# Issuing the first wave of loads without the three holds on SyncE's queue

## The chip, the core and the metric

The kernel runs on one core of one Trainium2 chip. Such a core has TensorE (PE, the matmul engine), VectorE (DVE), ScalarE (ACT), GpSimd (POOL) and SyncE (SP), which run side by side and wait for one another through semaphores, and 16 DMA engines that move the data. SP and ACT each issue loads on a queue of their own: q1 in the profile is SP's, q10 is ACT's. The metric is the time of one execution on the device in microseconds, as the median of several runs.

## The reference

One transformer layer on a sequence of 2048 rows of width 512, all in bf16:

```python
h = x + A(layernorm(x))          # A: attention over 8 earlier positions, 2 apart; 32 heads of 16
out = h + B(layernorm(h))        # B: (relu(h @ W_gate) * (h @ W_up)) @ W_down, F = 1376
```

In A, `x @ wqkv` gives queries, keys and values. Row s looks at the keys of the rows s, s-2, ..., s-14, takes a softmax over these eight, sums the values with it, and the result is multiplied with `wo`. The layernorms have no weights.

## The kernel before

The 2048 rows are cut into four chunks of 512 (`tk` 0 to 3), and a chunk into four blocks of 128 rows, so that x consists of 16 blocks, x_0 to x_15; chunk 1 is x_4 to x_7. Each chunk goes through the same stages:

- Layernorm. DVE takes the statistics of each of the four blocks (`bn_stats`, L468, and `bn_aggr`, L471). ACT makes the reciprocal deviation from them (L481, L485). For chunks 1 to 3 DVE makes a bias (L489) and ACT scales the four blocks (L500); for chunk 0 DVE scales (L503). TensorE transposes the blocks (L532) and ACT copies the transposed ones out of the accumulator banks (L548). In chunk 3 four DMA transposes on SP's queue do this instead (L521).
- Queries, keys and values. L573 multiplies the transposed chunk with the weights: 12 steps of four matmuls, for q, k and v and four tiles each. ACT casts the results from the banks to SBUF (L581). In chunk 0 the first six steps are cut into smaller parts, so that they can begin as soon as single blocks of x are there.
- Logits. DVE multiplies queries with shifted keys (L639 in chunk 0, in eight pieces; L624 in the others), TensorE sums over the width of a head (L630), ACT takes the exponential (L688), DVE masks the beginning of the sequence in chunk 0 (L691). SP broadcasts the weights over the partitions with eight DMAs per chunk (L748).
- Values. DVE multiplies them with the weights (L795 in chunk 0, L780 in the others) and adds up (L783 and the lines after it, with POOL's adding DMAs, L823). Then follow the output projection (L861, with `wo`), the second layernorm, the gated network (L934 with the gate and up weights, L984 with the down weights) and the store.

The chunks are interleaved: TensorE works on one chunk's matmuls while DVE works on the attention of another. The order is written out by hand. Each step is an `Op` with an engine, and `Plan.add` gives it the next entry of the list `RANK`; `Plan.order` sorts each engine's steps by rank, so the list fixes the order of the 758 steps on each engine. Every engine then goes through its own list in that order, and a step that waits holds up all the steps behind it. `XT` and `WT` are the times at which the planner believes the loads to land; with a written-out rank they do not change an engine's order, only the choice among the buffers of a kind.

What matters here is `setup` (L312). It first issues chunk 0's loads in turn on SP's and ACT's queue: x_0 and x_2 and the first and third quarter of the q and k weights on SP, x_1 and x_3 and the other two quarters on ACT (L318, L319). Then GpSimd builds small constants (L321 to L330). Then come three holds, and behind each of them loads on SP's queue:

```python
nc.gpsimd.tensor_copy(out=x_sm[0:1, BPC:2 * BPC, 0:1], in_=x_sm[0:1, 3, 0:BPC])
for j in range(BPC, 2 * BPC):
    nc.sync.dma_start(x_sm[:, j:j + 1, :], x_rows[:, j:j + 1, :])
```

The copy reads four elements of x_3 and writes one into each of x_4 to x_7. So it waits until x_3 has landed, and the loads of x_4 to x_7 (L335) wait for the copy, as they write the same places. The second hold (L336) reads the last quarter of the q and k weights and writes an element of the v weights, which holds the v weights' load (L337). The third (L338) reads x_7 and writes an element of x_8, which holds x_8 to x_11 and, behind them on the queue, x_12 to x_15 (L340), the output weights (L342) and the gate weights (L310, two halves). The up and down weights are issued much later, behind a hold of their own (L841).

One more rule of the program counts: its loads from SP and ACT take eight completion semaphores in turn. A load therefore is not issued before the load eight places ahead of it has landed.

Of the kernel before, what the change touches and what calls it, by code (L numbers as in the profile page):

```python
# [17 lines left out]
RANK = [  # L18
# [38 lines left out]
]  # L57


# [143 lines left out]
def kernel(  # L203
# [11 lines left out]
    nc = tc.nc  # L215
# [23 lines left out]
    BPC = CS // P  # L239
# [25 lines left out]
    x_sm = sb.tile([P, NTB, D], BF16, name="x_sm")  # L265
    wqk_sb = sb.tile([P, NT, 2 * D], BF16, name="wqk_sb")
    wv_sb = sb.tile([P, NT, D], BF16, name="wv_sb")
# [44 lines left out]
    def setup():  # L312

        w3_r = A_wqkv.rearrange("(dt p) f -> p dt f", p=P)
        for i in range(2):
            for n, q in enumerate((nc.sync, nc.scalar)):
                j = 2 * i + n
                q.dma_start(x_sm[:, j:j + 1, :], x_rows[:, j:j + 1, :])  # L318
                q.dma_start(wqk_sb[:, j:j + 1, :], w3_r[:, j:j + 1, 0:2 * D])  # L319
        nc.scalar.preload_act_table_set("natural_log_exp_and_others")  # L320
        V.memset(warm[:], 0.0)  # L321
        make_identity(nc, identity[:])
        nc.gpsimd.memset(eps_t[:], EPS)
        nc.gpsimd.iota(ci[:], pattern=[[0, 1]], base=0, channel_multiplier=1)
        nc.gpsimd.iota(sel_i[:], pattern=[[1, H]], base=0, channel_multiplier=0)
        nc.gpsimd.iota(sp_i[:], pattern=[[1, H], [0, DQ]], base=0, channel_multiplier=0)
        nc.gpsimd.iota(sm_i, pattern=[[0, 4], [1, H]], base=0, channel_multiplier=0)
        nc.gpsimd.iota(mk_i[:], pattern=[[1, PADL]], base=0, channel_multiplier=0)
        nc.gpsimd.memset(kT[:, :, 0:PADL], 0.0)
        nc.gpsimd.memset(vT[:, :, 0:PADL], 0.0)  # L330


        nc.gpsimd.tensor_copy(out=x_sm[0:1, BPC:2 * BPC, 0:1], in_=x_sm[0:1, 3, 0:BPC])
        for j in range(BPC, 2 * BPC):
            nc.sync.dma_start(x_sm[:, j:j + 1, :], x_rows[:, j:j + 1, :])  # L335
        nc.gpsimd.tensor_copy(out=wv_sb[0:1, 0, 0:1], in_=wqk_sb[0:1, 3, 0:1])  # L336
        nc.sync.dma_start(wv_sb[:], w3_r[:, :, 2 * D:3 * D])  # L337
        nc.gpsimd.tensor_copy(out=x_sm[0:1, 2 * BPC, 0:1], in_=x_sm[0:1, 2 * BPC - 1, 0:1])  # L338
        for tk in range(2, NCK):
            nc.sync.dma_start(x_sm[:, tk * BPC:(tk + 1) * BPC, :], x_rows[:, tk * BPC:(tk + 1) * BPC, :])  # L340

        nc.sync.dma_start(wo_sb[:], A_wo.rearrange("(p t) f -> p t f", t=NT))  # L342
        for n in "gud":
            for i in range(2):
                if n not in LATE:
                    f_load(n, i)


        for n, (op, by) in enumerate(((ALU.arith_shift_right, 2), (ALU.bitwise_and, H - 1),
                                      (ALU.arith_shift_right, 5))):  # L350
            V.tensor_scalar(out=tmp[:, n:n + 1], in0=ci[:], scalar1=by, scalar2=None, op0=op)
        V.tensor_copy(out=cf[:, 0:3], in_=tmp[:])
        V.tensor_scalar(out=cf[:, 2:3], in0=cf[:, 2:3], scalar1=1.0 * DIL, scalar2=None, op0=ALU.mult)
        V.tensor_scalar(out=cf[:, 3:4], in0=cf[:, 2:3], scalar1=4.0 * DIL, scalar2=None, op0=ALU.add)
        V.tensor_scalar(out=sel[:], in0=sel_i[:], scalar1=cf[:, 0:1], scalar2=None, op0=ALU.is_equal)
        V.tensor_scalar(out=spread[:], in0=sp_i[:], scalar1=cf[:, 1:2], scalar2=None, op0=ALU.is_equal)
        V.tensor_scalar(out=same[:], in0=sm_i, scalar1=cf[:, 1:2], scalar2=None, op0=ALU.is_equal)
        for hf in range(2):
            V.tensor_scalar(out=mask[:, hf, :], in0=mk_i[:], scalar1=cf[:, 2 + hf:3 + hf],
                            scalar2=None, op0=ALU.is_ge)  # L360
# [13 lines left out]
    NWARM, NFILL = 46, (8, 0, 0)  # L374
    NHALF = 6
    QA, QC = 6, 3
    XT = (3.5, 3.65, 5.6, 6.1, 8.5, 8.9, 9.4, 9.9, 15.9, 17.4)
    WT = (7.55, 7.55, 5.0, 14.2, 18.7, 25.5, 22.0, 29.0)
    DMAT = (('h',2,0),('h',2,2),('h',3,0),('h',3,2),('h',1,0),('x',3,0),('x',3,2))

    EARLY = (1, 2, 3)
# [689 lines left out]
```

## Time and profile before

| what | value |
|---|---|
| median of three runs (lowest to highest) | 196.97 us (196.93 to 197.28) |
| the profiled execution's own time | 197.36 us |
| its span, first to last instruction | 195.5 us |
| mean granted TensorE clock | 1.00 of full speed |
| busy: PE, DVE, ACT, POOL | 189.1, 147.2, 118.9, 18.6 us |
| read from and written to HBM | 8.42 MB, 2.10 MB |

All moments below are microseconds from the start of the span. What ends a matmul is modelled, so that "busy" on PE includes filling and draining; the pitch from one matmul to the next says how fast it works: 0.216 us for 512 columns, 0.056 us for 128. The profile gives for each load when it was issued and how long it took until it had landed:

| load | issued | landed | | load | issued | landed |
|---|---|---|---|---|---|---|
| x_1 (ACT) | 0.74 | 3.79 | | x_5 | 7.02 | 9.12 |
| x_0 | 0.74 | 3.62 | | x_6 | 7.49 | 9.98 |
| qk weights, 2nd quarter (ACT) | 1.17 | 5.02 | | x_7 | 7.97 | 12.33 |
| qk weights, 1st quarter | 1.21 | 4.71 | | v weights | 8.49 | 13.51 |
| x_3 (ACT) | 1.68 | 6.38 | | x_8 to x_11 | 12.66 | 16.17 |
| x_2 | 1.68 | 5.44 | | x_12 to x_15 | 13.09 | 17.58 |
| qk weights, 4th quarter (ACT) | 2.16 | 7.86 | | output weights | 13.64 | 20.10 |
| qk weights, 3rd quarter | 2.15 | 7.68 | | gate weights, two halves | 14.18, 14.66 | 21.80, 23.49 |
| x_4 | 6.64 | 8.72 | | | | |

### The profile page before, as it was taken

Reading aid. Unit: us, or ns where it says so; the run is one execution under the profiler, and the core shown is the slowest. Engines: PE = TensorE matmul, PEld = TensorE weight load, DVE = VectorE, ACT = ScalarE, POOL = GpSimd, SP = SyncE. Lnnn points to the kernel's source line nnn. Section 1 sums busy time; section 2 is a strip of 40 time slices with the busy share of each in tenths; the row PEclk is TensorE's granted clock in tenths of the full one; section 3 lists DMA queues with packets and bytes.
Section 4 is the critical chain, followed back from the end, with each engine's and each line's share of the span. In section 5 each row is a group of like instructions: output and inputs, shape, how many; then the busy total and the mean of one; then the engine's idle time right before and its main releaser. Section 6 shows DMA issues by size and latency. Waiting matters only on the chain.

```text
span 195.5 us, 3121 instructions
## 1 busy us (share of the span) xinstructions
PE 189.1 (97%) x1149; PEld 97.5 (50%) x1149; DVE 147.2 (75%) x237; ACT 118.9 (61%) x245; POOL 18.6 (10%) x34
## 2 busy tenths in 40 slices
PE   7998998899999999999999999999999999999993
PEld 7884453454445544454446444444445545544542
DVE  6969989999999899998997748999965410521432
ACT  3659997986798847674357658722579612364500
POOL 3000000600400013100032200013000000000000
PEclk9999999999999999999999999999999999999999
DMA  6759675795087919965359965226300540100044
GB/s 202 223 163 343 235 177 126 144 200 97 0 288 163 288 56 174 193 133 121 89 113 190 191 139 117 54 54 110 54 0 0 133 112 0 27 27 0 3 143 152
DMA packets 25214, 24.61 MB, mean 126 GB/s; under 512 B 11408, under 2 KB 21488, under 8 KB 25200
## 3 DMA queue, kind: packets, MB, share of 16 engines
q1 hardware_dynamic: 22176, 16.26, 30.7%
q0 software_dynamic: 2304, 7.34, 20.2%
q10 hardware_dynamic: 720, 0.82, 1.2%
q8 instruction: 9, 0.15, 0.4%
q14 instruction: 5, 0.04, 0.1%
HBM read 8.42 MB, written 2.10 MB: 54 GB/s over the span
## 4 chain that ended last, share of the span: by engine, by line
PE 80%; DVE 7%; DMA 7%; issue 1%; SPq 1%; ACT 1%; ACTq 0%; POOL 0%
PE bank L934 35%; PE bank L984 20%; PE bank L573 11%; PE bank L861 7%; DMA x_sm<-in_A_x_dram 5%; DVE big L639 4%; PE bank L630 3%; PE bank L901 3%; DVE st L468 2%; DMA quad<-row 1%; DMA big<-ex 1%; PE bank L532 1%; SPq L748 1%; SPq L335 1%; PE bank L864 0%
## 5 line engine op out<-in xcount | busy, mean ns | idle before, releaser
L934 PE MATMUL bank<-quad,wgu_sb 128*128 128x512 bf16 x320 | 71.9, 379 | 0.0
L934 PEld LDWEIGHTS <-wgu_sb 128*128 128x128 bf16 x320 | 31.0, 98 | 36.6 <-issue 0.8
L984 PE MATMUL bank<-wd_sb,gT 128*128 128x512 bf16 (+3 forms) x198 | 39.7, 355 | 0.0
L938 ACT CAST up_sb<-bank 128x512 bf16<-128x512 f32 x40 | 22.3, 594 | 17.6 <-PE bank L934 15.3
L573 PE MATMUL bank<-quad,wqk_sb 128*128 128x512 bf16 (+2 forms) x176 | 30.4, 321 | 0.3 <-DMA quad<-row 0.2
L941 ACT ACTIVATE gr<-bank 128x512 bf16<-128x512 f32 x40 | 23.6, 605 | 11.1 <-PE bank L934 9.0
L984 PEld LDWEIGHTS <-gT 128*128 128x128 bf16 (+1 forms) x198 | 18.3, 98 | 19.6 <-issue 0.4
L624 DVE TENSOR_TENSOR big<-quad,kT 128x4096 bf16<-128x4096 bf16 x12 | 27.4, 2288 | 0.8 <-ACT kT L581 0.6
L780 DVE TENSOR_TENSOR big<-big,vT 128x4096 bf16<-128x4096 bf16 x12 | 27.0, 2287 | 0.0
L962 DVE TENSOR_TENSOR gT<-gr,up_sb 128x1024 bf16<-128x1024 bf16 x20 | 13.4, 687 | 12.1 <-ACT up_sb L938 6.1
L573 PEld LDWEIGHTS <-wqk_sb 128*128 128x128 bf16 x176 | 16.9, 113 | 10.5 <-issue 1.0
L783 DVE TENSOR_TENSOR big<-big 128x1024 bf16<-128x1024 bf16 (+2 forms) x24 | 17.1, 731 | 0.4 <-DMA big<-big 0.2
L823 POOL DMA_DIRECT2D big<-big x12 | 10.5, 902 | 71.5 <-DVE big L780 48.2
L573 PE MATMUL bank<-quad,wv_sb 128*128 128x512 bf16 x64 | 15.5, 380 | 0.0
L861 PE MATMUL bank<-wo_sb,quad 128*128 128x512 bf16 x64 | 15.1, 379 | 0.0
L872 DVE SCALAR_TENSOR_TENSOR x_sm<-x_sm,bank 128x512 bf16<-128x512 bf16 x12 | 8.2, 687 | 6.3 <-PE bank L861 6.3
L468 DVE BATCH_NORM_STATS2 st<-x_sm 128x6 f32<-128x512 bf16 x16 | 10.3, 682 | 2.5 <-DMA x_sm<-in_A_x_dram 2.5
L548 ACT COPY quad<-bank 128x1024 bf16<-128x1024 bf16 (+1 forms) x10 | 8.7, 894 | 5.6 <-PE bank L532 5.6
L457 ACT ACTIVATE row<-x_sm,mv 128x512 bf16<-128x512 bf16 x12 | 8.6, 718 | 5.2 <-DVE mv L449 5.0
L997 DVE TENSOR_TENSOR row<-x_sm,bank 128x512 bf16<-128x512 bf16 (+2 forms) x10 | 5.5, 578 | 8.1 <-PE bank L984 6.2
L573 PEld LDWEIGHTS <-wv_sb 128*128 128x128 bf16 x64 | 7.0, 114 | 7.0 <-issue 1.3
L911 DVE TENSOR_TENSOR row<-gr,bank 128x192 bf16<-128x192 bf16 x8 | 2.7, 352 | 10.2 <-ACT gr L907 10.2
(76 smaller groups left out, 177.5 us busy)
## 6 DMA issues: line engine op xcount, KB each, us to landing
big<-big POOLq DMA_DIRECT2D x12, 512.0 KB, 5.5
big<-ex SPq DMA_DIRECT2D x32, 128.0 KB, 2.7
wgu_sb<-in_B_W_gate_dram SPq DMA_DIRECT2D x2, 688.0 KB, 8.2
wgu_sb<-in_B_W_up_dram SPq DMA_DIRECT2D x2, 688.0 KB, 4.7
wd_sb<-in_B_W_down_dram SPq DMA_DIRECT2D x2, 640.0 KB, 5.8
x_sm<-in_A_x_dram SPq DMA_DIRECT2D x2, 512.0 KB, 4.0
x_sm<-up_sb POOLq DMA_DIRECT2D x4, 256.0 KB, 4.6
out_dram<-x_sm SPq DMA_DIRECT2D x4, 256.0 KB, 2.3
```

What stands on the lines that cost most here:

```text
L468: V.bn_stats(out=st.t[:], in_=x_sm[:, tk * BPC + j, :])
L573: nc.tensor.matmul(mm.t[:, lo:hi], lhsT=wv_sb[:, dt, t:D:NT] if c == 2 else wqk_sb[:, dt, c * D + t:(c + 1) * D:NT], rhs=xnT.t[:, dt, lo:h ...
L624: V.tensor_tensor(out=pb.t[:].rearrange("p (t w) s -> p t w s", t=2), in0=q4, in1=k4, op=ALU.mult)
L780: V.tensor_tensor(out=mt.t[:], in0=ab.t[:], in1=v8, op=ALU.mult)
L783: V.tensor_tensor(out=mt.t[:, 0:n, :], in0=mt.t[:, 0:n, :], in1=mt.t[:, n:2 * n, :], op=ALU.add)
L823: nc.gpsimd.dma_start(mt.t[:, 0:4, :], mt.t[:, 4:8, :], accum_op=ALU.add)
L861: nc.tensor.matmul(od.t[:], lhsT=OT.t[:, t, j * P:(j + 1) * P], rhs=wo_sb[:, t, :], start=(t == 0), stop=(t == NT - 1 and tk not in RPE))
L934: nc.tensor.matmul(mm.t[:fs, lo:hi], lhsT=wgu_sb[:, dt, g, ft * P: ft * P + fs], rhs=hnT.t[:, dt, lo:hi], start=(dt == 0), stop=(dt == NT ...
L938: nc.scalar.copy(out=ub.t[:fs, i, :], in_=um.t[:fs, :])
L941: nc.scalar.activation(out=gr.t[:fs, i, :], in_=gm.t[:fs, :], func=ACT.Relu)
L962: V.tensor_tensor(out=gt.t[:fs, 0:n, :], in0=gr.t[:fs, 0:n, :], in1=ub.t[:fs, 0:n, :], op=ALU.mult)
L984: nc.tensor.matmul(od.t[:, c0:c1], lhsT=gts[ft].t[:fs, ft % 2, j * P:(j + 1) * P], rhs=wd_sb[:fs, ft, c0:c1], start=(ft == 0), stop=(ft == ...
```

## The change

The three holds are taken out, so that SP goes on to the loads of chunks 1 to 3, of the v, output and gate weights right behind chunk 0's, in the same order as before. The planner's landing times are set earlier, and `RANK` is written anew (the list is cut here):

```diff
@@ -18,42 +18,42 @@
 RANK = [
     0, 1, 2, 3, 4, 5, 6, 7, 8, 9, 10, 11, 12, 13, 14, 15, 16, 17, 18, 19,
     20, 22, 23, 25, 29, 30, 32, 21, 24, 26, 28, 31, 35, 38, 43, 27, 33, 36, 37, 48,
-    53, 58, 34, 41, 45, 49, 54, 59, 63, 44, 57, 95, 97, 98, 102, 47, 87, 91, 92, 94,
...
+    53, 58, 34, 41, 45, 49, 54, 59, 62, 47, 57, 94, 97, 98, 103, 44, 85, 89, 90, 95,
...
@@ -330,12 +330,9 @@
-        nc.gpsimd.tensor_copy(out=x_sm[0:1, BPC:2 * BPC, 0:1], in_=x_sm[0:1, 3, 0:BPC])
         for j in range(BPC, 2 * BPC):
             nc.sync.dma_start(x_sm[:, j:j + 1, :], x_rows[:, j:j + 1, :])
-        nc.gpsimd.tensor_copy(out=wv_sb[0:1, 0, 0:1], in_=wqk_sb[0:1, 3, 0:1])
         nc.sync.dma_start(wv_sb[:], w3_r[:, :, 2 * D:3 * D])
-        nc.gpsimd.tensor_copy(out=x_sm[0:1, 2 * BPC, 0:1], in_=x_sm[0:1, 2 * BPC - 1, 0:1])
         for tk in range(2, NCK):
             nc.sync.dma_start(x_sm[:, tk * BPC:(tk + 1) * BPC, :], x_rows[:, tk * BPC:(tk + 1) * BPC, :])
@@ -374,8 +371,8 @@
-    XT = (3.5, 3.65, 5.6, 6.1, 8.5, 8.9, 9.4, 9.9, 15.9, 17.4)
-    WT = (7.55, 7.55, 5.0, 14.2, 18.7, 25.5, 22.0, 29.0)
+    XT = (3.5, 3.65, 5.6, 6.1, 8.1, 8.5, 8.9, 9.4, 13.0, 14.5)
+    WT = (7.55, 7.55, 5.0, 11.5, 16.5, 25.5, 20.5, 29.0)
```

Counted through the calls of `add`, the new list puts 97 of TensorE's 242 steps, 47 of DVE's 213, 61 of ACT's 225, 17 of SP's 43 and none of POOL's 17 at another place in their engine's order, mostly by one to three places. In the first 35 us the moves are these. DVE takes the statistics of chunk 1 in the order x_5, x_7, x_4, x_6, before in the order x_4, x_5, x_6, x_7. ACT's first 51 steps stand as they were. On TensorE some parts of chunk 0's q and k steps change places, and chunk 1's four transpositions, which all stood behind the v steps of tiles 2, 1 and 3, now stand one before these three, one before the last of them and two behind. Later moves are swaps among steps of the same kind.

70 rows, old and new, of the table RANK are left out of this document.

## The prediction

> **What bounds the kernel now.** The page first: PE is busy 97% of the span at full granted clock. So the question is where PE still waits, and for what. The waits of PE between 5.7 and 36 us are short; from 36 to 192.3 us that view lists none. The rows of PE's timeline at its two holes:
>
> ```profile
> 14.61 2.75 PE L573 MATMUL bank<-quad,wv_sb 128*128 128x512 bf16 x12
> 17.79 1.10 PE L532 MATMUL bank<-identity,row 128*128 128x128 bf16 x12 [0.42 <-ACT row L500]
> 19.19 0.40 PE L532 MATMUL bank<-identity,row 128*128 128x128 bf16 x4 [0.30 <-ACT row L500]
> 19.52 1.05 PE L630 MATMUL bank<-big,sel 128*32 128x512 bf16 x16
> ...
> 30.72 2.75 PE L573 MATMUL bank<-quad,wqk_sb 128*128 128x512 bf16 x12
> 34.54 0.40 PE L532 MATMUL bank<-identity,row 128*128 128x128 bf16 x4 [1.07 <-ACT row L500]
> 35.16 1.03 PE L573 MATMUL bank<-quad,wqk_sb 128*128 128x512 bf16 x4 [0.22 <-DMA quad<-row]
> ```
>
> By pitch, the twelve at 14.61 end at 17.20 (12 x 0.216). From there to 19.52 lie 16 transpositions of 0.056, so 2.32 - 0.90 = 1.4 us are empty, 0.1 of it the usual step to L630. The twelve at 30.72 end at 33.31, and up to 35.16 only four transpositions (0.22) are done: 1.6 us empty. So PE idles 1.3 + 1.6 = **2.9 us** in all between 8.8 us and its end at 192.2. From 35.16 on it is full; if that moment comes d earlier, the end does. The chain of waits says what sets it:
>
> ```profile
> 1.68 4.70 DMA x_sm<-in_A_x_dram
> ...
> 6.43 0.20 POOL x_sm L333
> ...
> 6.64 0.33 SPq L335
> ...
> 7.97 4.37 DMA x_sm<-in_A_x_dram
> 12.33 0.02 issue
> 12.36 0.69 DVE st L468
> 13.05 0.28 DVE mv L471 x4
> ...
> 14.51 7.95 DVE big L639 x7
> 22.46 0.07 DVE ex L691
> ...
> 35.16 1.03 PE bank L573 x4
> ```
>
> Read downward: x_3 lands (6.38), the first hold lets go, four loads are issued, x_7 lands at 12.33, DVE takes its statistics, and only then, in DVE's order, the eight pieces of L639 run without a break to 22.46; mask, broadcasts, DMA transposes and chunk 2's layernorm follow, up to PE at 35.16. Ahead of x_7 DVE stands idle 1.66 us:
>
> ```profile
> 12.36 0.69 DVE L468 BATCH_NORM_STATS2 st<-x_sm 128x6 f32<-128x512 bf16 x1 [1.66 <-DMA x_sm<-in_A_x_dram]
> ```
>
> **The change, part by part.** *The three copies*: 0.19, 0.21 and 0.18 us on POOL, which has nothing else between 2.4 and 34.2 us: nothing gained by themselves.
>
> *When SP can issue.* SP is free at 2.58 and has no other work until L748 at 22.57, so moving eleven issues (0.33 to 0.50 us each) forward queues them past nothing. The limit of eight loads in flight remains; its effect is seen now in SP's waits, where L335 waits 1.2 us for a load of x before the 2.8 us for POOL. So x_4 goes when x_1 has landed (3.8), x_5 at 4.3, x_6 after 5.02, x_7 at 5.5, the v weights after x_3 (6.4), x_8 at 6.9, x_12 after 7.86, the output weights at 8.4, the gate weights near 9. "Not held back" is thus only partly true, but x_7 goes 2.5 us earlier.
>
> *When x_7 lands.* It stands behind chunk 0's quarters on q1, whose packets run out between 6.5 and 7.6 us; the queue is nearly empty between 6.5 and 7.5 us now (mean 76 GB/s). With full queues the same 1-KB packets ran at 382 GB/s (14.6 to 16.5 us). The four loads are 0.52 MB, 1.4 us. From 7.6, the slowest engine's time, plus 0.2 us from last packet to landing (x_4 now): 9.2. From 6.6: 8.2. Above, if the train takes as long as it does now (first packet 7.6, landing 12.33: 4.7 us) behind chunk 0's last landing at 7.86: 12.6. I take 9.2, since with descriptors queued ahead the late row (16 engines busy throughout) is the nearest; 8.2 and 12.6 stay as ends.
>
> *DVE.* Free at 8.46. In the new order x_7 stands second: its statistics start at 9.2, those of x_4 and x_6 follow at a pitch of 0.6 (three in 1.88 us now), the last starts at 10.4, and from a last start to L639 it takes 13.25 - 12.36 = 0.89: L639 could start at 11.3. Its first piece needs two casts of L581, the second of which ends near 11.15 (the pair from 10.60 takes 1.08). So 11.3 against 13.25: **1.9 us** earlier; the casts allow 2.0 at most.
>
> *Does the rest keep up?* ACT waits 1.69 us for the aggregation before 13.37; it would do L481 at 11.7, its next two casts by 13.3 and the next one by 14.6, and L639's third and fourth pieces need these at 13.7 and 14.8. So L639 ends near 20.5, not 22.46. ACT finishes chunk 1's four scalings near 17.8 (19.1 now); PE, with transpositions now mixed into the v steps, reaches the last of them at 17.9 and L630 at 18.1: the hole of 1.3 closes. The exponential that L691 needs comes near 20.2, so the broadcasts start at 20.7, 1.8 earlier than 22.57. SP's own issues set what follows (eight of 0.55 to 1.3 us, four transposes of 1.2 to 1.3), so the last transposed block lands at 35.03 - 1.8 = 33.2. PE, 1.3 earlier at 32.0, waits there: of the second hole 1.1 stays. PE is full from 33.35 instead of 35.16.
>
> *The other loads.* The v weights land by about 13 even if they lose as much as x_7 did, and PE needs them at 14.8; x_8 to x_15 by about 16, needed after 20.6; the output and gate weights are needed after 50 us. Nothing gained, nothing late.
>
> *The rank.* Past 35 us PE waits for nothing now, and DVE, which feeds it, comes earlier by the same 1.8. The 97 moved PE steps do the same work; a new wait costs what it lasts, bounded below by nothing and above by the gain as far as I can tell. I take 0.
>
> **Sum**: -1.8 us. The profiled execution took 197.36 (195.5 of span, 1.9 around it), so 195.5 on its own scale; the median of the runs is 0.4 lower than it: 196.97 - 1.8 = **195.2 us**.
>
> [...] Between 6.5 and 7.5 us ACT's q10 still moves 34 packets of chunk 0 and q1 only 21: SP's queue runs dry first. [...]
>
> **The rivals.**
>
> 1. *x_7 lands late again (slower).* x_7 took 4.37 us, x_4 to x_6 2.1 to 2.5: the profile has the other engines through by 10.0 and one 2.3 us behind, while an instruction fetch of 16 KB (queue q8, 0.95 us) starts at 10.32. DVE's new order has two more statistics behind x_7's, so the break-even is a landing at 13.25 - 0.89 - 1.2 = 11.1. At 12.6, L639 starts at 14.7, 1.4 later: 198.4; at 11.9, 197.7, which I take. For it: the new order hangs more work on the last block. Against it: my x_7 is through a microsecond before the fetch.
>
> 2. *Half the gain.* If x_4 to x_7 share turns with chunk 0's last loads, x_3 is late by up to 1.4 us, with a cover of only 0.18 (it lands at 6.38, DVE takes it at 6.56). Its casts, and with them L639, then start near 12.4: 0.8 gained, 196.2. The same comes out if x_7 lands near 10.2. Against it: x_4 to x_6 landed in order of issue.
>
> 3. *No change.* The gain at 35 us is eaten by a new wait further on, where the rank is new: 197.0. Against it: not one wait of PE past 36 us now, though that says nothing of how near the next one is.
>
> **How the numbers follow.** Forecast 195.2, with its own range of 194.6 (all but 0.6 of the 2.9 us) to 195.7: 0.58. Half the gain (195.8 to 196.5): 0.14. No change: 0.11. Slower by the late x_7: 0.17. A measurement of this kernel can tell about 0.2% (0.4 us) from no change, so: faster 0.72, same 0.11, slower 0.17. From 194.6 to 197.1 the range holds the first two cases and most of the third, about 0.8.
>
> **What would show it.** In the changed kernel's profile: x_4 issued near 3.8 and x_7 near 5.5; x_7 landed by 9.6; x_3 and the quarters still at 6.4 and 7.9; DVE's L639 from 11.3; PE without a hole between 17 and 19.5 and one of about 1.1 us near 32 to 33.4; no wait of PE after that. The forecast falls if x_7 lands after 10.5, if chunk 0's loads move, or if PE waits past 34 us.

## The result, and the profile after

Nine executions of the changed kernel took 195.35 to 196.46 us, median 196.27; nine of the kernel before, in turn with them, 196.41 to 197.57, median 196.93. The ratio is 0.9954, with an interval of 0.9934 to 0.9974: faster by half a percent, 0.7 us by the medians (0.0046 x 196.93 = 0.9 by the ratio). The two profiled executions say more: 195.35 against 197.36, so 2.0 us; but 195.35 is the shortest of the nine. (Ratios leave out an execution more than 1.5% above the fastest of its kernel; medians and lists hold all.)

The profiled execution has a span of 193.4 us, PE busy 187.9 us (97%), and PE's last matmul is through at 190.41 by pitch (its start plus 0.056), where before it was 192.21: 1.80 us earlier. The other 0.2 of the 2.0 us lie behind that matmul. The landings, from the issues of the trace: x_4 to x_7 are issued at 3.64, 4.02, 5.05 and 5.43 and land at 8.23, 8.52, 8.85 and 9.30; x_3 lands at 6.27, the last two quarters of the q and k weights at 7.80 and 8.02; the v weights at 11.41, the output weights at 17.74. The chain of waits of the changed kernel up to 36 us (start, length, what), whose L465, L636 and L570 are the old L468, L639 and L573:

```profile
1.17 3.87 DMA wqk_sb<-in_A_wqkv_dram
...
5.05 0.33 SPq L334
5.38 0.04 issue
5.43 3.88 DMA x_sm<-in_A_x_dram
9.30 0.02 issue
9.33 1.88 DVE st L465 x3
...
12.74 7.95 DVE big L636 x7
...
33.37 1.03 PE bank L570 x4
```

No hold stands in it any more. What releases x_6's issue at 5.05 is the landing of a quarter of weights, eight loads before it. x_7 is there at 9.30, and three statistics stand behind its landing (its own and two more), where before only its own did. PE's timeline of the same execution at the places of the old holes:

```profile
16.80 1.03 PE L570 MATMUL bank<-quad,wv_sb 128*128 128x512 bf16 x4
17.67 0.61 PE L529 MATMUL bank<-identity,row 128*128 128x128 bf16 x8
18.21 1.05 PE L627 MATMUL bank<-big,sel 128*32 128x512 bf16 x16
...
29.38 2.75 PE L570 MATMUL bank<-quad,wqk_sb 128*128 128x512 bf16 x12
32.35 0.40 PE L529 MATMUL bank<-identity,row 128*128 128x128 bf16 x4 [0.21 <-ACT row L497]
33.37 1.03 PE L570 MATMUL bank<-quad,wqk_sb 128*128 128x512 bf16 x4 [0.62 <-DMA quad<-row]
```

Four v matmuls end at 17.66, eight transpositions follow at once, then the logits: the first hole is gone. The twelve at 29.38 end at 31.97; up to 33.37 four transpositions are done, so 1.2 us of the second hole stay. After that PE waits for nothing, as before. In this execution the mechanism is as predicted, nearly to the tenth. The open question was the rest: why the median gains 0.7 us and not 1.8.

### The profile page after: what moved, and what is told of

Its sections match the earlier page's. It is cut to its first block, busy times and chain, and to the rows that moved or that the text cites. A ratio compares the mean times of both kernels' runs of the same rounds, so it can differ in the third digit from the quotient of the medians.

```text
span 193.4 us, 3112 instructions
## 1 busy us (share of the span) xinstructions
PE 187.9 (97%) x1149; PEld 96.9 (50%) x1149; DVE 147.5 (76%) x237; ACT 118.8 (61%) x245; POOL 18.1 (9%) x31
## 4 chain that ended last, share of the span: by engine, by line
PE 81%; DVE 8%; DMA 6%; SPq 1%; issue 1%; ACT 1%; ACTq 0%
PE bank L931 36%; PE bank L981 20%; PE bank L570 11%; PE bank L858 7%; DVE big L636 4%; PE bank L627 3%; PE bank L898 3%; DVE st L465 2%; DMA x_sm<-in_A_x_dram 2%; DMA wqk_sb<-in_A_wqkv_dram 2%; DMA quad<-row 1%; PE bank L529 1%; DMA big<-ex 1%; SPq L745 1%; DVE big L792 0%
## 5 line engine op out<-in xcount | busy, mean ns | idle before, releaser
L570 PE MATMUL bank<-quad,wqk_sb 128*128 128x512 bf16 (+2 forms) x176 | 30.2, 321 | 0.7 <-DMA quad<-row 0.6
L570 PEld LDWEIGHTS <-wqk_sb 128*128 128x128 bf16 x176 | 17.0, 114 | 11.1 <-issue 1.4
L570 PE MATMUL bank<-quad,wv_sb 128*128 128x512 bf16 x64 | 15.7, 380 | 0.0
L465 DVE BATCH_NORM_STATS2 st<-x_sm 128x6 f32<-128x512 bf16 x16 | 10.3, 680 | 0.5 <-DMA x_sm<-in_A_x_dram 0.3
L578 ACT CAST quad<-bank 128x512 bf16<-128x512 f32 x16 | 9.1, 600 | 1.8 <-PE bank L570 1.6
L570 PEld LDWEIGHTS <-wv_sb 128*128 128x128 bf16 x64 | 6.8, 114 | 6.6 <-issue 1.3
```

The costliest lines, as they stand in the source:

```text
L465: V.bn_stats(out=st.t[:], in_=x_sm[:, tk * BPC + j, :])
L570: nc.tensor.matmul(mm.t[:, lo:hi], lhsT=wv_sb[:, dt, t:D:NT] if c == 2 else wqk_sb[:, dt, c * D + t:(c + 1) * D:NT], rhs=xnT.t[:, dt, lo:h ...
```

## The experiments

The theories changed on the way, and each expectation names its own. In short: **A / theory 1**, the holds cost through x_7's landing, which varies from one execution to the next, and the profiled execution of before was one with a late x_7; **theory 2**, in the changed kernel chunk 0's own blocks decide; **B**, a new wait late in the kernel. Twelve runs follow, eight of them of edited kernels. In the table, "start" is the first of the eight pieces of the logits' products on DVE (L639, or its number in that kernel); the time is that of the profiled execution itself, and matmuls end by pitch.

| profiled execution | x_2 lands | x_3 lands | x_7 lands | start | PE's last matmul ends | end less start | own time |
|---|---|---|---|---|---|---|---|
| before | 5.44 | 6.38 | 12.33 | 13.25 | 192.21 | 178.96 | 197.36 |
| before, again | 5.76 | 5.54 | 9.56 | 11.45 | 190.71 | 179.26 | 195.86 |
| before, third | 6.12 | 6.91 | 12.54 | 13.46 | 192.67 | 179.21 | 197.86 |
| before, without x_7 | 5.48 | 6.57 | 12.06 | 11.67 | 190.81 | 179.14 | 195.99 |
| order alone | 6.14 | 6.94 | 12.48 | 14.65 | 194.24 | 179.59 | 199.43 |
| first hold kept | 7.00 | 7.74 | 13.35 | 15.52 | 194.48 | 178.96 | 199.48 |
| loads alone | 7.26 | 8.07 | 10.20 | 14.28 | 194.04 | 179.76 | 199.05 |
| after | 5.54 | 6.27 | 9.30 | 11.48 | 190.41 | 178.93 | 195.35 |
| after, again | 7.01 | 7.81 | 9.96 | 12.77 | 192.48 | 179.71 | 197.44 |
| after, third | 7.01 | 8.07 | 10.14 | 12.84 | 192.48 | 179.64 | 197.60 |
| after, chunk 1 free | 6.59 | 5.65 | 9.16 | 12.36 | 191.38 | 179.02 | 196.45 |
| after, chunk 0 free | 7.05 | 8.04 | 10.09 | 12.25 | 190.92 | 178.67 | 195.96 |
| first hold dropped alone | 6.67 | 6.87 | 9.37 | 12.43 | 191.35 | 178.92 | 196.61 |
| x first | 4.01 | 4.25 | 10.33 | 12.49 | 191.40 | 178.91 | 196.49 |

PE's end follows the start by 178.7 to 179.8 us in all fourteen, while the start itself moves by 4 us. Most of what decides the time thus lies before that start. The rest can be placed too: from the L573 matmuls that wait for the last block out of the DMA transposes (33.37 after, 35.16 before; L570 to L573 by kernel) to PE's end it is 157.05 us in every one of the fourteen, within 0.02, with the old order and with the new. So theory B falls: nothing behind that moment varies. The 1.1 us by which the difference does vary lie between the start and that moment; why was not followed up.

**The changed kernel again** (no edit).

> The changed kernel once more, with a second profile. Two theories of why the median fell by only 0.7 us where the two profiled executions differ by 2.0. Theory A (the landing varies): what differs from one execution to the next is when x_7 lands; the start of L636 on DVE then follows x_7, and PE's last matmul follows that start one to one. By A an execution of 196.3 us shows x_7 near 10.2 instead of 9.30 and the first L636 near 12.4 instead of 11.48, and one of 195.4 shows 9.3 and 11.5. Theory B (a later wait): the loads land alike in all executions (x_7 within 0.2 us of 9.30), and the slower executions have a wait of PE of about 0.8 us after 34 us, which the first profile did not have. The time is expected at 195.3 to 196.5 with a median near 196.2 by both.

Measured: median 196.13 (195.29 to 197.44), ratio 0.9969 (0.9942 to 0.9997). The profiled execution is its longest, 197.44, and it is the first to show what theory A had not foreseen. x_7 lands at 9.96, early enough; but x_2 lands at 7.01 and x_3 at 7.81, where the first profile had 5.54 and 6.27. DVE's timeline of this execution, and below it pieces of its chain of waits:

```profile
7.03 0.69 DVE L465 BATCH_NORM_STATS2 st<-x_sm 128x6 f32<-128x512 bf16 x1 [1.52 <-DMA x_sm<-in_A_x_dram]
7.64 0.40 DVE L500 TENSOR_SCALAR row<-x_sm,mv,rs 128x512 bf16<-128x512 bf16 x1
...
9.85 2.46 DVE L465 BATCH_NORM_STATS2 st<-x_sm 128x6 f32<-128x512 bf16 x4
...
12.77 1.23 DVE L636 TENSOR_TENSOR big<-quad,kT 128x2048 bf16<-128x2048 bf16 x1
```

```profile
1.68 5.33 DMA x_sm<-in_A_x_dram
...
7.64 0.40 DVE row L500
...
12.18 0.50 ACT kT L578
12.72 0.04 issue
12.77 0.06 DVE big L636
```

DVE waits 1.52 us for x_2, and behind it in its order stands the scaling of x_1 (L500), for which everything is there: PE waits 1.69 us for that. The four statistics of chunk 1 then run without a wait, so x_7 no longer counts; the start comes with chunk 0's casts, whose second ends near 12.7 instead of the 11.15 worked out. The chain says the same: it begins with the landing of x_2 at 7.01 and goes through the scaling of x_1 and the casts to the start. Theory A is half right: the start decides, but not x_7 alone.

**The kernel before again** (no edit).

> The kernel before once more, for a second profile and as a measure of the comparison itself: ratio 1.000 within 0.002. By theory A x_7 lands at another time than 12.33 when the execution takes another time than 197.36: 0.5 us earlier for 196.9. By theory B x_7 lands at 12.3 again, and what differs lies after 35 us.

Measured: median 196.51 (195.84 to 198.16), ratio 0.9985 (0.9956 to 1.0015). The same kernel beside it had a median of 196.99, so medians of one kernel lie half a microsecond apart here; differences of that size between two kernels say little by themselves. (The changed kernel's gain rests on its two intervals, which both leave out 1.) The profiled execution took 195.86. x_3 landed at 5.54, the held loads went from 5.80 on, and x_7 landed at 9.56; DVE's timeline has no wait there:

```profile
8.60 2.46 DVE L468 BATCH_NORM_STATS2 st<-x_sm 128x6 f32<-128x512 bf16 x4
10.98 0.36 DVE L471 BATCH_NORM_AGGREGATE mv<-st 128x2 f32<-128x6 f32 x4
11.45 1.23 DVE L639 TENSOR_TENSOR big<-quad,kT 128x2048 bf16<-128x2048 bf16 x1
```

With all its holds the kernel before starts at 11.45, as early as the changed one at its best. So x_7 at 12.33 is not what the holds bring always; they bring it in some executions.

**The loads alone.** The edit: the three copies out, `RANK`, `XT` and `WT` as before.

> The three holds out, the order of all engines and the planner's times as before. x_7 lands near 9.3 as in the changed kernel, and DVE takes x_7's statistics last, so L639 starts at 11.3. If the loads are the whole of the gain, 196.2 us as the changed kernel (both theories); if the new order is worth something by itself, more: chunk 1's transpositions stand behind all v steps, so PE should keep a hole of 0.3 us near 17.5, and the second hole shrinks by as much; no change in the end. I expect 196.2, within 0.4.

Measured: median 197.10 (195.43 to 199.74), ratio 0.9988 (0.9957 to 1.0019): no gain to be told where 196.2 was expected, and times spread over 4 us. The profiled execution, at 199.05 the second longest of the twelve, has x_2 and x_3 at 7.26 and 8.07 and a second loss on top. PE stood idle for 1.92 us, up to 8.35, for the scaling of x_1. The windows of this trace show (stretch, length, busy time of PE, its weight loads, DVE, ACT and POOL, granted clock, DMA share, GB/s):

```profile
6.00:8.30 2.30, 0.43 (x8) 0.25 (x5) 1.02 (x4) 0.59 (x1) 0.00 (x0) 0.98 0.97 351
8.30:11.60 3.30, 3.25 (x31) 3.26 (x32) 3.27 (x9) 1.26 (x5) 0.00 (x0) 0.50 0.63 191
```

The granted clock is 0.50 from 8.22 to 11.63. The 18 small matmuls of L570 in that stretch take 2.13 us, where the changed kernel's second profile has 1.45 for them at a granted clock of 1.00; the start is 14.28, with x_7 there since 10.20. Its mean granted clock is 0.991. Of the executions without a trace here only that mean is on record. With this one, seven have 0.991 or less: two each of this kernel and of the order alone, one each of the first hold kept, x first and before without x_7. All executions of the changed kernel and of the kernel before for which it was noted have 0.997 or more. Whether the loads without the new order are worth less than with it stays open, as the intervals of this kernel and of the changed one overlap.

**The order alone.** The edit: the changed kernel's `RANK`, `XT` and `WT` in the kernel before, holds kept.

> The three holds kept, the order and the planner's times of the changed kernel. DVE's new order has x_7 second among chunk 1's four statistics, so two more stand behind its landing at 12.3: L639 starts 1.2 us later than 13.25, and the time is 197.0 + 1.2 = 198.2 us (both theories). If the order were worth something by itself beside the loads, it would be less than 197.8.

Measured: median 196.60 (195.52 to 200.72), ratio 0.9969 (0.9938 to 1.0001). The expectation failed: 1.6 us too high. Its mechanism is there in the profiled execution (199.43), on DVE's timeline:

```profile
9.89 0.69 DVE L468 BATCH_NORM_STATS2 st<-x_sm 128x6 f32<-128x512 bf16 x1 [0.83 <-DMA x_sm<-in_A_x_dram]
12.51 1.88 DVE L468 BATCH_NORM_STATS2 st<-x_sm 128x6 f32<-128x512 bf16 x3 [1.92 <-DMA x_sm<-in_A_x_dram]
...
14.65 1.20 DVE L639 TENSOR_TENSOR big<-quad,kT 128x2048 bf16<-128x2048 bf16 x1
```

x_7 at 12.48, three statistics behind it, the start 1.2 us after the 13.46 that the old order made of x_7 at 12.54. But most executions of this kernel are not like that one: nine of the twelve took 198.01 or less, and the 200.03 and 200.72 have a mean clock of 0.991 besides. How often x_7 is late in the kernel before is not shown; two of its three profiles caught it. One rival stays: this ratio is that of the changed kernel beside it (0.9969 in both), and the loads alone have 0.9988. So the times do not tell whether the loads or the order bring the gain. Against the order speak this trace, where it costs 1.2 us, and the mean of all twelve, 197.4 against 197.0 of the kernel before beside it.

**The changed kernel and the kernel before, third profiles** (no edit; one execution each).

> A third profile of the changed kernel. The theories now. Theory 1: the profiled execution of before was one with a late x_7 (12.33, where another one had 9.56), so the usual gain of the earlier issue is smaller than 1.8. Theory 2: without the holds chunk 0's own loads land late in part of the executions (x_3 at 7.81 where the first profile had 6.27, the last quarter of the q and k weights at 8.87 for 8.02), and this takes back part of the gain. By theory 2 an execution of 196.1 us or more shows x_3 after 6.9, one of 195.5 or less shows it before 6.5; x_7 is before 10.1 in both. Without theory 2 x_3 is before 6.9 in any execution.

Measured: 197.60, with x_2 at 7.01, x_3 at 8.07, x_7 at 10.14, and the start at 12.84: theory 2's pattern.

> A third profile of the kernel before. By theory 1 an execution near 197 us shows x_7 after 11, one of 196.3 or less before 10.5, with x_3 before 7.0 in both. By theory 2 alone x_7 is near 12.3 whenever, and the time varies for another reason.

Measured: 197.86, with x_2 at 6.12, x_3 at 6.91, x_7 at 12.54 and the start at 13.46: theory 1's pattern.

**The first hold kept.** The edit, in the changed kernel:

```diff
+        nc.gpsimd.tensor_copy(out=x_sm[0:1, BPC:2 * BPC, 0:1], in_=x_sm[0:1, 3, 0:BPC])
         for j in range(BPC, 2 * BPC):
```

> The changed kernel with the first hold put back alone: x_4 to x_7 wait for x_3, the v weights and all behind them follow without further holds. Chunk 0 then has the queues to itself up to 6.4 us, as in the kernel before, but the v weights stand right behind x_7. By theory 2 the late executions vanish: x_3 lands before 7.0, x_7 near 9.6, L637 starts near 11.6 and the median is 195.7. By theory 1 x_7 is late in part of the executions (after 11), as with the holds, and DVE's order has it second: median 196.6 or more.

Measured: median 196.86 (196.04 to 199.48), against 196.72 of the kernel before beside it; ratio 1.0032 (0.9990 to 1.0073). The gain is gone, as theory 1 says. That the first hold alone takes it is not shown by this: with the new order a late x_7 has two more statistics behind it, and the first hold dropped alone (below) gained nothing clear of the noise. Theory 2's own forecast (195.7, no late block of chunk 0) failed doubly: in the profiled execution (199.48) x_2 landed at 7.00 and x_3 at 7.74 although nothing stood behind them on the queues until x_3 was there. Late blocks of chunk 0 also come with the first hold.

**x first.** The edit: chunk 0's loads in two rounds, first the four blocks of x, then the four quarters.

```diff
                 q.dma_start(x_sm[:, j:j + 1, :], x_rows[:, j:j + 1, :])
+        for i in range(2):
+            for n, q in enumerate((nc.sync, nc.scalar)):
+                j = 2 * i + n
                 q.dma_start(wqk_sb[:, j:j + 1, :], w3_r[:, j:j + 1, 0:2 * D])
```

> The changed kernel with chunk 0's four blocks of x issued before its four quarters of weights (x_0, x_2 on SP, x_1, x_3 on ACT, then the quarters). x_2 and x_3 then stand in front of 0.5 MB less and land near 4.7, 1.9 us before DVE wants x_3; the first two quarters land near 5.9 instead of 5.0, before their use at 6.85, and the last two as now, near 8. By theory 2 the executions with a late x_3 vanish, and what is left is a late last quarter, first used at 8.8: median 195.6 or less. By theory 1 alone it changes nothing: 196.2.

Measured: median 196.44 (195.63 to 198.48), ratio 0.9997 (0.9962 to 1.0032). x_2 and x_3 land at 4.01 and 4.25, but all four quarters at 7.52 to 9.14, the first two 1.6 to 1.8 us later than I worked out. The 195.6 that theory 2 forecast did not come. In the profiled execution the start, 12.49, does not come by way of the late weights either: the second cast of L581 ends near 11.7, but DVE waits 1.23 us for a block of chunk 1 (x_5, 9.62), and x_7 lands at 10.33 with three statistics behind it. No version to keep.

**Before, without x_7.** The edit, in the kernel before:

```diff
-                        V.bn_stats(out=st.t[:], in_=x_sm[:, tk * BPC + j, :])
+                        V.bn_stats(out=st.t[:], in_=x_sm[:, tk * BPC + (0 if (tk, j) == (1, 3) else j), :])
```

> The kernel before, but the fourth statistic of chunk 1 is taken of x_4 a second time and not of x_7 (so x_7 is normalised with wrong numbers); every load and hold stays. DVE then waits for no later load than x_6. Theory 1 (the holds cost through x_7's late landing, and only through it): the start of L639 comes to 11.4 to 12.0, PE's last matmul 179.2 us after it, and the median falls to that of the changed kernel, 196.2, from 196.9. If x_7's landing is not the way, it stays at 196.9.

Measured: median 196.06 (195.79 to 199.26), against 196.62 of the kernel before beside it; ratio 0.9977 (0.9952 to 1.0001). Ten of the twelve lie below 196.45, of the kernel before 15 of 35. For the way of the wait this is the decisive one: the profile caught a late x_7 again, 12.06, and it does no harm:

```profile
8.99 2.48 DVE L468 BATCH_NORM_STATS2 st<-x_sm 128x6 f32<-128x512 bf16 x4 [0.47 <-DMA x_sm<-in_A_x_dram]
11.38 0.37 DVE L471 BATCH_NORM_AGGREGATE mv<-st 128x2 f32<-128x6 f32 x4
11.67 1.19 DVE L639 TENSOR_TENSOR big<-quad,kT 128x2048 bf16<-128x2048 bf16 x1
```

With the dependence in place, x_7 at 12.06 would have meant a start near 12.97 (0.02 to the statistics and 0.89 from there, as in the kernel before); it is 11.67. So a late x_7 moves the start through its statistics, and only through them. What this is worth in the median is not sharp: 0.6 us by the medians, 0.5 by the ratio, and the interval reaches 1.

**After, chunk 1 free.** The edit, in the changed kernel: `in_=x_sm[:, (0 if tk == 1 else tk) * BPC + j, :]` in the same line.

> The changed kernel, with all four statistics of chunk 1 taken of chunk 0's blocks (chunk 1 is normalised with wrong numbers); every load stays. No landing of chunk 1 stands between chunk 0 and L636 any more. Theory 2 (in the changed kernel chunk 0's own loads decide, not x_7): nothing changes, 196.2, and the start of L636 follows the casts of chunk 0: 11.3 when x_3 lands near 6.3, 12.8 when it lands near 8. If x_7 still decided, 0.3 us or more would be gained: below 195.9.

Measured: median 196.20 (195.07 to 196.96), ratio 0.9968 (0.9938 to 0.9998): near the changed kernel's 196.13 and 196.27, which were not measured beside it. No landing of chunk 1 can be seen to cost it anything any more. The profiled start, 12.36, follows x_2, which landed at 6.59, and not x_3, which landed at 5.65.

**After, chunk 0 free.** The edit, in the changed kernel: `tk * BPC + (j % 2 if tk == 0 else j)` in that line, and the same, for the first layernorm, in the line that picks the block to scale, so that x_0 and x_1 stand in for x_2 and x_3 there.

> The changed kernel, with chunk 0's blocks x_2 and x_3 replaced by x_0 and x_1 in the first layernorm (statistics and scaling; the first layernorm of these two blocks is wrong); every load stays. A late x_2 or x_3 then holds up nothing before the residual at 50 us. Theory 2: the executions that were slow by a late x_2 or x_3 vanish, PE's hole at 6.2 to 8 us is below 0.5 us in the profile, the start of L636 is 11.3 to 12.0, and the median is 195.6, with nine of ten executions within 0.5 us. If chunk 0's loads are not what spreads the times: 196.2 as the changed kernel.

Measured: median 195.69 (194.97 to 196.41), against 196.62 of the kernel before; ratio 0.9951 (0.9927 to 0.9976). That is half a microsecond below the kernel with chunk 1 free, which ran beside it, and near the 195.6 expected; but the changed kernel's own ratios, 0.9954 and 0.9969, lie in this interval, so the size of the gain is not shown. In the profiled execution x_2 and x_3 are as late as 7.05 and 8.04, and PE's hole there, 1.85 us by pitch in the changed kernel's second profile, is 0.24. The spread shrinks less than I wrote: nine of twelve within 0.5 us of the median, not nine of ten. DVE now waits for chunk 1's blocks (x_5 at 9.42, a wait of 1.18), and the start is 12.25, above the 11.3 to 12.0 expected: with x_2 out of the way, theirs is the next lateness.

**First hold dropped alone.** The edit: the second and third copy back in the changed kernel.

> The changed kernel with the second and third hold put back: only the first hold is gone, x_4 to x_7 are issued as early as in the changed kernel, the v weights wait for the last quarter and x_8 for x_7. Theory 1: the first hold is the whole cost, so this takes 196.2 as the changed kernel. If the second and third cost as well, 196.5 or more.

Measured: median 196.44 (195.39 to 197.33), ratio 0.9988 (0.9954 to 1.0022). Between the changed kernel's 196.1 to 196.3 and the 196.62 of the kernel before beside it: it does not tell whether the second and third hold cost anything. Its profile has x_7 at 9.37 as the changed kernel has.

## Why the prediction was right, and where it was wrong

The direction was right, and the measured 196.27 lies in the range of 194.6 to 197.1. That range was wide enough to hold even no change (197.0). The likeliest value, 195.2, missed by 1.1 us, and its own range ended at 195.7; what came is the number of the second rival, half the gain, at 196.2.

*When SP can issue, when x_7 lands, DVE, the two holes*: right in the profiled execution (5.5 and 5.43 for the issue; 9.2 and 9.30 for the landing; 11.3 and 11.48; PE full from 33.35 and 33.37; 1.80 us gained at PE's end). That it fits so closely is in part luck: this was the shortest of nine executions, and the next two profiles of the same kernel start at 12.77 and 12.84. *The other loads, the rank*: right for what lies behind the second hole; PE waits for nothing there, with either order. Ahead of it DVE's new order does count when x_7 is late (1.2 us in the profile of the order alone). *"x_3 and the quarters still at 6.4 and 7.9"*: in the first profile x_3 landed at 6.27 and ACT's last quarter at 8.02; in the next two x_3 landed at 7.81 and 8.07, and that quarter at 8.87 and 8.79. What delayed the quarter there was not looked at.

*"The profiled execution took 197.36 ... the median of the runs is 0.4 lower than it"* is the step that failed. I took the difference off both kernels as if it were a constant around the span. It was a sign that the profiled execution was not the usual one: its x_7 at 12.33, on which the whole 1.9 us rests, is one way in which that kernel runs; with x_7 at 9.56 it takes 195.86. In the table start and own time differ by 183.7 to 184.8 us, 184.3 in the mean, so that the median of 196.93 stands for a start near 12.6, give or take 0.5, not 13.25. No profile of before lies within 0.4 us of its median, so what the usual one waits for is not shown.

*"Its first piece needs two casts of L581, the second of which ends near 11.15"*: taken as fixed, and it moves with x_2. In four profiles without the first hold (after again, after third, chunk 1 free, first hold dropped alone) the start comes 5.76 to 5.83 us behind x_2's landing, whether x_3 landed at 5.65 or at 8.07, and the chain of waits of each begins with x_2's load. DVE takes x_2's statistics first, and the scaling of x_1 stands behind them; x_3's turn comes a microsecond later. The median of 196.27 stands for a start near 12.0, by the same 184.3, not 11.3. That is the second rival's price, but the block that it named, x_3 with its cover of 0.18 us, is not the one in these profiles. In the profile before, x_2 landed at 5.44 and was taken at 5.56, a cover of 0.12.

Why x_2 is late is not shown. Without the first hold (x first left aside) it landed at 5.54, 6.59, 6.67, 7.01, 7.01, 7.05 and 7.26; with it, at 5.44, 5.48, 5.76, 6.12, 6.14 and 7.00. It looks as if the new loads delayed it, but the ranges overlap, and in the last of these nothing stood behind it on the queues until x_3 had landed. That stays open.

*The slower rival*, a late x_7, did not come: x_7 landed at 9.2 to 10.3 in all eight profiles without the first hold, however late chunk 0 was. With that hold it landed after 12 in five of six.

## What to carry to other kernels

One profile is one execution. Where its own time differs from the median, find out which landing made it so before its waits are priced; here the second profile of the kernel before showed x_7 at 9.56 and a start as early as the changed kernel's best. When a load is freed, ask what the engine waits for next, and whether that too moves from one execution to the next: here x_7's late landings went and x_2's stayed. And on an engine that goes through its steps in order, a step for which all is there should not stand behind one that waits for a load; here DVE's scaling of x_1 stands behind the statistics of x_2, which costs PE 1.7 us in the profile where x_2 landed at 7.01 (another order was not tried).

## What the runs showed of the hardware

*The instruction fetch and x_7.* In the five profiles in which x_7 landed after 12, the first fetch of instructions (16 KB in one packet, queue q8) began between 9.41 and 10.55, while x_7's packets were on their way, and took 0.95 to 1.53 us on one of the 16 DMA engines. Where it began at 11.8, in the kernel before's second profile, x_7 landed at 9.56. One exception speaks against a simple cause: with chunk 0 free, the fetch began at 9.02 and took 1.81 us, and x_7 landed at 10.09. That the fetch holds up one engine, and with it the block, is thus possible and not shown. A kernel in which the fetch falls at another time was not tried.

*The clock.* In the profile of the loads alone PE was idle for 1.92 us, up to 8.35 us, and the granted clock was 0.50 for 3.41 us from 8.22 on; the idle stretch of 1.69 us in the changed kernel's second profile brought no such fall: its granted clock is 1.00 in all windows up to 14 us. No other profiled execution has a mean granted clock below 0.997 (0.991 here), so one profile shows the fall; what brought it about, and what set its length, is not shown.
